# Batch 0 of an attention and maxout-FFN kernel: softmax sums inverted together on ScalarE, value bursts and three loads moved

## The chip, the cores and the metric

The kernel runs on 1 core of a Trainium2 chip. The metric is the device time of one execution in microseconds. The kernel before took 287.16 us, the median of 3 runs (286.48 to 287.23). One more execution was taken with the hardware profiler; every row of a profile shown here comes from that execution.

## The reference

```python
B, H, S, Nb, D = 8, 8, 576, 16, 64               # batches, heads, tokens, beacons, head size
k_all = concat([beacon_k, k], axis=2)            # 592 keys: 16 beacons, then the tokens
v_all = concat([beacon_v, v], axis=2)
scores = q @ k_all.T / sqrt(D)
scores = where(causal, -1e9, scores)             # beacons are seen by every query
a = softmax(scores)
attn = a @ v_all
x = attn.transpose(0, 2, 1, 3).reshape(4608, 512)
h = maximum(maximum(x @ w1, x @ w2), x @ w3)     # 512 -> 768
out = h @ w_out                                  # 768 -> 512
```

Inputs and output are float32; the kernel multiplies in bfloat16.

## The kernel before

Heads go in pairs, 4 pairs per batch, 32 pairs in all. Two pairs make a quad (4 heads), two quads a batch. The queries and keys of a pair are transposed on TensorE (`turn_part` by halves of 288 tokens in batch 0, `turn_pair` whole afterwards), each transposition into a PSUM bank that another engine copies to `qT` and `kT`. `emit_scores` multiplies keys by queries for one of four groups of key tiles and query ranges; ScalarE turns the group into exponentials in `at_sb`; `emit_masks` clears what lies above the diagonal, on VectorE or on GpSimd (POOL). `emit_pv` makes a value burst of one quad and one half of its queries: pass 0 multiplies the exponentials by ones, which gives the softmax sums, passes 1 to 3 multiply them by the even and odd columns of the values, for each of the five key tiles that the half sees. `invert_sums` makes 1/sum and `multiply` writes sum-normalised columns to `xT`, the input of the FFN. The FFN works in units; its first six are each a 256-column half of the first 512 tokens for two of six blocks of `w1`, and `emit_ffn` lets a unit through only when its tokens are in `xT`.

There is no scheduler: the order in which the Python calls stand is the order on each engine. An engine works through its own instructions in that order, and an instruction that waits holds up everything behind it. The order of batch 0 is written out by hand in `first_batch`, with `S_` for scores, `T` for a half transposition (its last argument is a number of filler matmuls of 512 columns put in front), `M` for masks (True: on VectorE), `P` for a value burst, `V` for the cast of a value tile, `F` for FFN units.

PSUM has eight banks in batch 0: scores take banks 0, 1 and 2, 3 in turn (`sc_psum`), value bursts banks 4 and 5 (`pv_psum`), FFN units banks 6 and 7 (`ffn_psum`); `emit_pv(..., apart=True)` takes the FFN's two banks, `tiles=` takes a pair of score banks. The transpositions of batch 0 name their banks 4 to 7 themselves.

Loads without a cast are issued on SyncE's queue (SP). `load_cast` (a pair of heads, as bfloat16), `load_w(i)` (FFN weight number i of three, from 0, in two halves) and `load_w_out` are issued by POOL, in its order among casts and masks, and use a DMA queue of their own. Five value tiles of 128 keys (the last of 80) come on SP's queue, issued at L306; `cast_first_v` (`V`, L334) casts each on POOL. `second_batch` goes through pairs 4 to 7, in the same way but with whole bursts of scores, and issues `load_cast(8)`, `load_w_out` and `load_cast(9)` on the way; pair 8 is transposed at its end.

Lines that the prediction speaks of: L247, L334, L277 and L322 casts, L258 `load_cast`, L344 `load_w`, L415 filler matmuls, L427 half transpositions, L435 their copies, L505 scores of batch 0 and L514 their exponentials, L558 and L560 masks on VectorE and POOL, L609 the value bursts of batch 0, L678 the reciprocal on VectorE, L680 and L681 the inversion on ScalarE (logarithm, then exponential of its negative), L691 the products, L750 and L764 the first FFN units and their casts or maxima.

Of the kernel before, what the change touches and what calls it, by code (L numbers as in the profile page):

```python
# [11 lines left out]
AF = mybir.ActivationFunctionType  # L12
# [5 lines left out]
def kernel(  # L18
# [13 lines left out]
    nc = tc.nc  # L32
# [4 lines left out]
    scale = 1.0 / float(D) ** 0.5  # L37
# [13 lines left out]
    HALF = S // 2  # L51
# [9 lines left out]
    PPB = H // 2  # L61
# [76 lines left out]
    sc_psum = Banks(0, 2, 2)  # L138
# [115 lines left out]
    def load_cast(p):  # L254
        b, g, j0 = place(p)
        for i, src in enumerate((q, k)):
            t16 = quads[g][i][:, 2 * j0 : 2 * j0 + 4]
            nc.gpsimd.dma_start(  # L258
                out=t16.rearrange("p (h s) r d -> p h (s r d)", h=2),
                in_=src[b, head(g, j0) : head(g, j0) + 2].rearrange("h (p r) d -> p h (r d)", r=QR),  # L260
            )
            rows = t16.rearrange("p (h s) r d -> p h (s r) d", h=2)
            stage["pair16", p, i] = (rows[:, 0], rows[:, 1])
# [26 lines left out]
    def load_v(b, piece, gate=None):  # L290
        st = new_stage(("v", b, piece))
        if gate:
            gate.memset(st[:, 0:1], 0.0)
        t_lo, t_hi = V_PIECES[piece]
        for t in range(t_lo, t_hi):
            i = t - t_lo
            dst = st[:, i * H * D : (i + 1) * H * D].rearrange("p (h d) -> p h d", h=H)
            lo = 0
            if t == 0:
                lo = Nb  # L300
                nc.sync.dma_start(
                    out=dst[0:Nb], in_=beacon_v[b].rearrange("h n d -> n h d")
                )
            t0 = k_tok[t] + lo
            n = k_rows[t] - lo
            nc.sync.dma_start(  # L306
                out=dst[lo : lo + n], in_=v[b, :, t0 : t0 + n, :].rearrange("h p d -> p h d")
            )
# [32 lines left out]
    def load_w(i, gs=range(n_quad)):  # L341
        wv = (moe_w1, moe_w2, moe_w3)[i].rearrange("(g p e) f -> g p e f", g=n_quad, e=2)
        for g in gs:
            nc.gpsimd.dma_start(out=w_in[i][:, 2 * g : 2 * g + 2], in_=wv[g])  # L344
# [6 lines left out]
    def load_beacons(b0, b1, dst, queue=None):  # L351
        for b in range(b0, b1):
            (queue or nc.sync).dma_start(
                out=dst[Nb * (b - b0) : Nb * (b - b0 + 1)],
                in_=beacon_k[b].rearrange("h n d -> n h d"),
            )

    def turn_beacons(b0, b1, src):
        n = Nb * (b1 - b0)
        ps = sc_psum.tile(BF16)[:, 0, 0 : PPB * n].rearrange("p (i n) -> p i n", i=PPB)  # L360
        for pi in range(PPB):
            nc.tensor.transpose(
                ps[:, pi],
                src[:, 2 * pi : 2 * pi + 2].rearrange("p h d -> p (h d)"),
                ident[0:n, 0:n],
            )
        if b0 == 0:
            by_act(kTs[0][:, 0:Nb], ps[:, 0, 0:Nb])
        by_act(bT[:, :, Nb * b0 : Nb * b1], ps)
# [43 lines left out]
    def fill(at_bank, n):  # L413
        for _ in range(n):
            nc.tensor.matmul(  # L415
                acc[:, at_bank], busy[:, 0:128], busy, start=True, stop=True
            )
# [162 lines left out]
    unfinished = []  # L580
# [87 lines left out]

        return finish

    def invert_sums(dve=False):
        if not unfinished:
            return
        quad, hf = unfinished.pop(0)
        ps = pv_tiles.pop((quad, hf))
        recip = nrm_pool.tile([128, S], FP32, name="recip")[:, 0:HALF]
        if dve:
            nc.vector.reciprocal(recip, ps[0][:, 0:HALF])  # L678
        else:
            nc.scalar.activation(out=recip, in_=ps[0][:, 0:HALF], func=AF.Ln)  # L680
            nc.scalar.activation(out=recip, in_=recip, func=AF.Exp, scale=-1.0)  # L681
        for n in range(1, NPASS):
            products.append((quad, hf, n, ps, recip))

    def multiply(count=NPASS):
        for _ in range(min(count, len(products))):
            quad, hf, n, ps, recip = products.pop(0)
            b, g = divmod(quad, n_quad)
            c0 = b % RING * S + hf * HALF
            part, bank, lo, ca, cb = passes[hf][n]  # L690
            nc.vector.tensor_mul(  # L691
                xT[:, 2 * g + part - 1, c0 + ca : c0 + cb],
                ps[bank][:, lo : lo + cb - ca],
                recip[:, ca:cb],
            )
            if g == n_quad - 1 and n == NPASS - 1:
                ready[0] = 2 * b + hf

    def finish_pv():
        invert_sums()  # L700
        multiply()

    hTs = {}
    MID = TOKB // 2
# [127 lines left out]
    def emit_ffn(limit, new_ps=ffn_psum.tile, close=False):  # L834
        if not may_emit(limit):
            return False
        need, fn, args = units[done[0]]
        done[0] += 1
        fn(*args, new_ps, *([True] if close else []))
        return True  # L840
# [72 lines left out]
    S_, T, M, P, V = emit_scores, turn_part, emit_masks, emit_pv, cast_first_v  # L913

    def F(n=1, new_ps=ffn_psum.tile, close=False):
        for _ in range(n):
            assert emit_ffn(END, new_ps, close)

    def first_batch():
        S_(0, 0)  # L920
        T(2, 0, 0, 6)
        T(3, 0, 0, 4)
        load_v(0, 0, nc.vector)
        load_v(0, 1)
        load_beacons(1, B_PE, bk32_1)
        S_(1, 0)
        T(2, 0, 1, 7)
        T(3, 0, 1, 5)
        M(0, 0, True)
        S_(2, 0)  # L930
        T(0, 1, 0, 6, None, 2)
        T(1, 1, 0, 4)
        S_(3, 0)
        T(0, 1, 1, 7, None, 2)
        T(1, 1, 1, 5)
        M(1, 0, True)
        S_(0, 1)
        V(0)
        T(2, 1, 0, 6, None, 2)
        T(3, 1, 0, 4)  # L940
        S_(1, 1)
        M(2, 0, True)
        V(1)
        load_w(0, [0])
        T(2, 1, 1, 7, None, 2)
        T(3, 1, 1, 5)
        M(3, 0, True)
        S_(0, 3)
        V(2)
        load_w(0, [1])  # L950
        S_(0, 2)
        fill(6, 2)
        S_(1, 3)
        for p in range(PPB):
            M(p, 1)
        M(0, 3, True)
        M(0, 2, True)
        V(3)
        V(4)
        load_w(1, [0])  # L960
        S_(1, 2)
        fill(6, 2)
        S_(2, 1)
        M(1, 3, True)
        M(1, 2, True)
        S_(3, 1)
        P(0, 0)
        invert_sums(True)
        multiply()
        S_(2, 3)  # L970
        load_w(1, [1])
        M(2, 3)
        P(1, 0, apart=True)
        invert_sums(True)
        multiply()
        S_(2, 2)
        M(2, 2)
        S_(3, 3)
        M(3, 3, True)
        P(0, 1, 0, 2)  # L980
        S_(3, 2)
        P(0, 1, 2)
        M(3, 2, True)
        by_pool(bk16_1, bk32_1)
        load_cast(PPB)
        load_cast(PPB + 1)
        load_cast(PPB + 2)
        load_w(2)
        load_cast(PPB + 3)
        invert_sums()  # L990
        multiply()
        P(1, 1, tiles=sc_psum.tile())
        invert_sums()
        F()
        multiply()
        F(2)
        turn_beacons(1, B_PE, bk16_1)
        place_beacons(PPB, by_act)
        F(2)
        free_banks[:] = [4, 5, 0, 1, 2, 3, 7, 6]  # L1000
        turn_pair(PPB, by_act)
        load_v(1, 0, nc.vector)
        load_v(1, 1)
        F(1, next_psum)

    def second_batch():
        for p in range(PPB, 2 * PPB):
            place_beacons(p + 1, by_act)
            emit_burst(p)
            if p == PPB + 1:  # L1010
                load_cast(2 * PPB)
            if p == PPB + 2:
                load_w_out()
                load_cast(2 * PPB + 1)
            for gi in range(NG):
                emit_masks(p, gi)
                if p == PPB + 2 and gi == 1:
                    cast_v(1, 0, by_pool)
            if p == PPB + 2:
                next_load(gate=nc.gpsimd)  # L1020
                next_load(4)
                cast_v(1, 1, by_pool)
            if p + 1 < 2 * PPB:
                turn_pair(p + 1, by_dve)
                F(2, next_psum)
                if p < PPB + 2:
                    F(1, last_pair(), True)
        F(2, next_psum)
        finish = emit_pv_whole(n_quad)
        turn_pair(2 * PPB, by_dve)  # L1030
        F(2, next_psum)
        finish()
# [93 lines left out]
```

## Time and profile before

| what | value |
|---|---|
| median of 3 runs | 287.16 us |
| the profiled execution | 286.96 us |
| its span, first to last instruction | 285.3 us |
| granted TensorE clock | 1.00 |
| TensorE busy, 9.04 to 14.43 us | 5.39 of 5.39 us |
| TensorE busy, 14.43 to 17.57 us | 2.32 of 3.14 us |
| TensorE busy, 17.57 to 22.16 us | 3.69 of 4.59 us |
| TensorE busy, 22.16 to 25.81 us | 2.73 of 3.65 us |
| TensorE busy, 25.81 to 30.86 us | 4.89 of 5.05 us |

The five stretches run from the third score group of batch 0 to the first transposition of pair 4. Columns of a timeline row: start in us from the span's start, length in us, engine, line, operation, output and input, partitions by elements, count, and in brackets the idle time of the engine before it with what ended it. PE is TensorE, PEld its weight loads, DVE is VectorE, ACT is ScalarE. Rows of one kind that follow each other closely are merged (x12 and the like), so a merged row's length is that of the whole run. Landing times are counted from the start of a DMA's issue to the arrival of its last part. q0 is the DMA queue of POOL's loads, q1 that of SP's.

### The profile page before, as it was taken

How to read it: one execution, taken by the hardware profiler on the slowest of the kernel's cores; microseconds unless marked ns; L12 is line 12 of the kernel's file. 1: busy time of each engine (PE TensorE's matmuls, PEld its weight loads, DVE VectorE, ACT ScalarE, POOL GpSimd, SP SyncE). 2: the span in 40 equal slices, each digit the busy share in tenths (PEclk: the TensorE clock that was granted, in tenths of full speed). 3: DMA queues.
4: the chain of work that ended last, by engine and by line, in shares of the span. 5: the costliest groups of instructions: out<-in, count | busy, mean ns of one | idle time of the engine just before them, and what ended most of it. 6: DMA issues, size and time to landing. Idle time of an engine off the chain costs nothing.

```text
span 285.3 us, 7780 instructions
## 1 busy us (share of the span) xinstructions
PE 275.6 (97%) x3079; PEld 157.6 (55%) x3079; DVE 177.3 (62%) x313; ACT 158.7 (56%) x295; POOL 134.4 (47%) x277
## 2 busy tenths in 40 slices
PE   7978999899999999999999999999999999999994
PEld 3447774555556555555556787555555554444442
DVE  3887675564774748373836384638364847776872
ACT  3893568885668585858585857576766640000000
POOL 7076479348386774557465836584336210000000
PEclk9999999999999999999999999999999999999999
DMA  8979999999995999999999999999861003103004
GB/s 138 207 128 184 206 219 195 229 219 289 274 165 145 241 268 228 165 252 267 240 179 231 250 238 224 179 217 237 138 177 70 0 2 112 38 0 147 2 0 147
DMA packets 85316, 48.84 MB, mean 171 GB/s; under 512 B 64416, under 2 KB 80032, under 8 KB 85280
## 3 DMA queue, kind: packets, MB, share of 16 engines
q1 hardware_dynamic: 78176, 42.22, 66.7%
q0 software_dynamic: 6544, 5.80, 13.3%
q8 instruction: 24, 0.39, 0.6%
q10 hardware_dynamic: 560, 0.33, 0.5%
q14 instruction: 12, 0.10, 0.1%
HBM read 35.13 MB, written 14.22 MB: 173 GB/s over the span
## 4 chain that ended last, share of the span: by engine, by line
PE 81%; DVE 1%; issue 1%; DVEq 0%
PE acc L721 45%; PE acc L773 16%; PE acc L642 11%; PE acc L520 7%; PE acc L406 2%; PE acc L791 0%; DVE hT L739 0%; DVE y L798 0%; DVE qT L442 0%; DVE kT L453 0%; DVEq L453 0%
## 5 line engine op out<-in xcount | busy, mean ns | idle before, releaser
L721 PE MATMUL acc<-xT,w_sb 128*128 128x512 bf16 (+4 forms) x744 | 135.5, 338 | 0.1
L739 DVE TENSOR_TENSOR hT<-hT,acc 128x512 bf16<-128x512 bf16 x102 | 69.9, 687 | 58.6 <-PE acc L721 53.7
L721 PEld LDWEIGHTS <-w_sb 128*128 128x128 bf16 x744 | 69.2, 98 | 59.6
L560 POOL TENSOR_SCALAR_AFFINE_SELECT at_sb<-at_sb 128x256 bf16<-128x256 bf16 (+1 forms) x171 | 62.2, 385 | 81.3 <-ACT at_sb L538 81.1
L538 ACT ACTIVATE at_sb<-acc 128x208 bf16<-128x208 f32 (+3 forms) x140 | 89.5, 735 | 6.8 <-PE acc L520 5.5
L773 PE MATMUL acc<-w_out_sb,hT 128*128 128x512 bf16 (+2 forms) x246 | 48.4, 348 | 0.0
L780 DVE COPY y<-acc 128x512 f32<-128x512 f32 (+1 forms) x35 | 22.0, 629 | 21.9 <-PE acc L773 15.7
L277 POOL CAST p<-st 96x768 bf16<-96x768 f32 x44 | 35.0, 824 | 0.0
L773 PEld LDWEIGHTS <-hT 128*128 128x128 bf16 x246 | 22.6, 98 | 21.7 <-DVE hT L739 1.6
L741 ACT CAST hT<-acc 128x352 bf16<-128x352 f32 x18 | 8.1, 452 | 47.0 <-PE acc L721 47.0
L741 DVE CAST hT<-acc 128x512 bf16<-128x512 f32 (+1 forms) x48 | 26.6, 554 | 9.5 <-PE acc L721 9.3
L520 PE MATMUL acc<-qT,kT 64*128 64x208 bf16 (+1 forms) x336 | 26.6, 280 | 0.5 <-DVE hT L764 0.2
L798 ACT COPY y<-acc 128x320 f32<-128x320 f32 x1 | 0.4, 426 | 46.0 <-PE acc L791 46.0
L642 PE MATMUL acc<-at_sb,v_sb 128*32 128x512 bf16 (+5 forms) x672 | 23.0, 281 | 0.6 <-issue 0.6
L520 PEld LDWEIGHTS <-kT 64*128 64x128 bf16 x336 | 15.4, 94 | 12.7 <-issue 2.6
L665 DVE TENSOR_TENSOR xT<-raw,recip 128x576 bf16<-128x576 f32 x28 | 21.1, 795 | 0.0
L642 PEld LDWEIGHTS <-v_sb 128*32 128x32 bf16 (+1 forms) x672 | 14.7, 96 | 7.4 <-issue 0.7
L322 POOL CAST v_sb<-st 128x1536 bf16<-128x1536 f32 (+2 forms) x21 | 18.3, 896 | 0.0
L652 ACT COPY raw<-acc 128x512 f32<-128x512 f32 x28 | 15.8, 633 | 2.6 <-PE acc L642 2.4
L642 PE MATMUL acc<-at_sb,ones 128*32 128x512 bf16 (+3 forms) x336 | 14.9, 284 | 0.0
L514 ACT ACTIVATE at_sb<-acc 128x1024 bf16<-128x1024 f32 (+2 forms) x16 | 13.2, 864 | 3.1 <-PE acc L505 3.1
L453 DVE COPY kT<-acc 128x576 bf16<-128x576 bf16 x12 | 9.0, 753 | 5.7 <-PE acc L406 4.5
(74 smaller groups left out, 181.8 us busy)
## 6 DMA issues: line engine op xcount, KB each, us to landing
out_dram<-y SPq DMA_DIRECT2D x35, 256.0 KB, 3.6
st<-in_q_dram SPq DMA_DIRECT2D x22, 288.0 KB, 4.3
st<-in_k_dram SPq DMA_DIRECT2D x22, 288.0 KB, 4.5
st<-in_v_dram SPq DMA_DIRECT2D x24, 256.0 KB, 6.4
w_sb<-in_moe_w_dram POOLq DMA_DIRECT2D x6, 384.0 KB, 7.7
q_dram<-p SPq DMA_DIRECT2D x16, 144.0 KB, 2.3
k_dram<-p SPq DMA_DIRECT2D x16, 144.0 KB, 2.2
st<-in_v_dram SPq DMA_DIRECT2D x8, 224.0 KB, 5.6
```

Of the source, the lines that this page charges most:

```text
L277: cast(t16.rearrange("p r h d -> p h r d"), st[0:QP, i * NQ2 : (i + 1) * NQ2].rearrange("p (h r d) -> p h r d", h=2, r=QR),)
L322: cast(v_sb[0:n, t:t1].rearrange("p t h d -> p (t h d)"), st[0:n, (t - t_lo) * H * D : (t1 - t_lo) * H * D],)
L520: nc.tensor.matmul(ps, kTs[p % NT][hs, 128 * t : 128 * t + 128], qTs[p % NT][hs, q0:q1], start=True, stop=True, tile_position=(64 * e, 0),)
L538: nc.scalar.activation(out=both_heads(p, gi)[:, e0:e1], in_=acc[:, first + e0 : first + e1, 0 : g_width(p, gi)], func=AF.Exp, scale=scale,)
L560: nc.gpsimd.affine_select(out=view, in_=view, compare_op=ALU.is_ge, fill=0.0, base=x0, pattern=[[0, 2], [1, hi - lo]], channel_multiplier=-1,)
L642: nc.tensor.matmul(acc[32 * j : 32 * j + 32, bank, lo + q0 - qa : lo + qb - qa], lhsT, at_view(PPQ * quad + j // 2, t, j % 2, q0, qb), sta ...
L665: nc.vector.tensor_mul(xT[:, 2 * g + i, c0 : c0 + S], raw[:, i], recip)
L721: nc.tensor.matmul(ps[:, a:b], w_in[i][:, ct, 128 * ft : 128 * (ft + 1)], xT[:, ct, x0 : x0 + b - a], start=(ct == 0), stop=(ct == n_ct - 1),)
L739: nc.vector.tensor_max(h[:, lo:hi], h[:, lo:hi], ps[:, lo:hi])
L741: (by_act if hi < TOKB else by_dve)(h[:, lo:hi], ps[:, lo:hi])
L773: nc.tensor.matmul(ps[:, lo:hi], hT[:, ft, 128 * tt : 128 * (tt + 1)], w_out_sb[:, ft, lo:hi], start=(ft == 0), stop=(ft == n_ft - 1),)
L780: (by_act if hi < d_model else by_dve)(y[:, lo:hi], ps[:, lo:hi])
```

## The change

`invert_sums` loses its choice of engine and takes the quad and half it is to invert; it always uses ScalarE. All four inversions of batch 0, each with its products on VectorE, stand at the end of the batch, in the order (quad 0, half 0), (1, 0), (0, 1), (1, 1); the first FFN unit stands after the third. Before, (0, 0) and (1, 0) were inverted by VectorE's reciprocal directly behind their value bursts, (0, 1) and (1, 1) by ScalarE.

Quad 0's first value burst uses the FFN's two banks, its second banks 4 and 5; quad 1's two bursts stand behind all scores and use the two pairs of score banks. The second burst of quad 0 starts in front of the last-but-one score group and not behind it. Four transpositions of batch 0 have one filler matmul in front where they had two. The two halves of `load_w(0)` are asked one place sooner each, in front of the casts V(1) and V(2); the two of `load_w(1)` move among calls of other engines. `load_cast(8)` moves from pair 5's turn to pair 6's, ahead of `load_w_out`.

```diff
-    def invert_sums(dve=False):
-        if not unfinished:
-            return
-        quad, hf = unfinished.pop(0)
+    def invert_sums(quad, hf):
+        unfinished.remove((quad, hf))
         ps = pv_tiles.pop((quad, hf))
         recip = nrm_pool.tile([128, S], FP32, name="recip")[:, 0:HALF]
-        if dve:
-            nc.vector.reciprocal(recip, ps[0][:, 0:HALF])
-        else:
-            nc.scalar.activation(out=recip, in_=ps[0][:, 0:HALF], func=AF.Ln)
-            nc.scalar.activation(out=recip, in_=recip, func=AF.Exp, scale=-1.0)
+        nc.scalar.activation(out=recip, in_=ps[0][:, 0:HALF], func=AF.Ln)
+        nc.scalar.activation(out=recip, in_=recip, func=AF.Exp, scale=-1.0)
...
-        T(0, 1, 0, 6, None, 2)
+        T(0, 1, 0, 6, None, 1)
         T(1, 1, 0, 4)
         S_(3, 0)
-        T(0, 1, 1, 7, None, 2)
+        T(0, 1, 1, 7, None, 1)
...
         V(0)
-        T(2, 1, 0, 6, None, 2)
+        T(2, 1, 0, 6, None, 1)
         T(3, 1, 0, 4)
+        load_w(0, [0])
         S_(1, 1)
         M(2, 0, True)
         V(1)
-        load_w(0, [0])
-        T(2, 1, 1, 7, None, 2)
+        load_w(0, [1])
+        T(2, 1, 1, 7, None, 1)
...
         V(2)
-        load_w(0, [1])
...
         V(4)
-        load_w(1, [0])
         S_(1, 2)
...
         S_(3, 1)
-        P(0, 0)
-        invert_sums(True)
-        multiply()
+        load_w(1, [0])
+        P(0, 0, apart=True)
         S_(2, 3)
         load_w(1, [1])
         M(2, 3)
-        P(1, 0, apart=True)
-        invert_sums(True)
-        multiply()
         S_(2, 2)
         M(2, 2)
+        P(0, 1, 0, 2)
         S_(3, 3)
         M(3, 3, True)
-        P(0, 1, 0, 2)
+        P(0, 1, 2)
         S_(3, 2)
-        P(0, 1, 2)
         M(3, 2, True)
...
         load_cast(PPB + 3)
-        invert_sums()
-        multiply()
+        P(1, 0, tiles=sc_psum.tile())
         P(1, 1, tiles=sc_psum.tile())
-        invert_sums()
-        F()
-        multiply()
+        for quad, hf in ((0, 0), (1, 0), (0, 1), (1, 1)):
+            invert_sums(quad, hf)
+            multiply()
+            if (quad, hf) == (0, 1):
+                F()
         F(2)
...
-            if p == PPB + 1:
+            if p == PPB + 2:
                 load_cast(2 * PPB)
-            if p == PPB + 2:
                 load_w_out()
                 load_cast(2 * PPB + 1)
```

More of the change, by code (lines that the diff above doesn't have):

```diff
@@ L697, in multiply @@
                 ready[0] = 2 * b + hf
-    def finish_pv():
-        invert_sums()
-        multiply()
     hTs = {}
@@ L989, in first_batch @@
         load_cast(PPB + 3)
-        invert_sums()
-        multiply()
+        P(1, 0, tiles=sc_psum.tile())
         P(1, 1, tiles=sc_psum.tile())
-        invert_sums()
-        F()
-        multiply()
+        for quad, hf in ((0, 0), (1, 0), (0, 1), (1, 1)):
[3 more added lines that the diff above has]
+                F()
         F(2)
```

## The prediction

> **What bounds the kernel now.** First the page: its engine rows and the chain that ended last.
>
> ```profile
> PE 275.6 (97%) x3079; PEld 157.6 (55%) x3079; DVE 177.3 (62%) x313; ACT 158.7 (56%) x295; POOL 134.4 (47%) x277
> PE 81%; DVE 1%; issue 1%; DVEq 0%
> ```
>
> TensorE is busy 275.6 of 285.3 us, and by the view of waits its matmuls wait 1.0 us in all after 31 us, never for a DMA. From there the kernel is a row of matmuls that starts when batch 0 lets it start; the change edits batch 0 and one load behind it, so I read its timeline. In the first half:
>
> ```profile
> 11.85 0.60 PE L415 MATMUL acc<-busy 128*128 128x512 bf16 x2
> 11.96 1.02 ACT L514 ACTIVATE at_sb<-acc 128x1024 bf16<-128x1024 f32 x1 [0.21 <-PE acc L505]
> 12.38 0.45 PE L427 MATMUL acc<-ident,quad 96*64 96x96 bf16 x12
> 12.76 0.39 PE L505 MATMUL acc<-qT,kT 64*128 64x288 bf16 x4
> 13.19 1.02 ACT L514 ACTIVATE at_sb<-acc 128x1024 bf16<-128x1024 f32 x1 [0.21 <-PE acc L505]
> ```
>
> Columns: start, length, engine, line. One step (two fills, 12 transposes, one score group) takes TensorE 13.19 - 11.96 = 1.23 us; the exp takes 1.02 and waits 0.21 for TensorE. TensorE sets this pace, with filler matmuls in it. In the second half:
>
> ```profile
> 18.31 1.96 DVE L678 RECIPROCAL recip<-acc 128x288 f32<-128x288 f32 x1 [0.38 <-PE acc L609]
> 20.26 0.39 PE L505 MATMUL acc<-qT,kT 64*128 64x288 bf16 x4 [0.46 <-ACT at_sb L514]
> 21.06 0.68 PE L609 MATMUL acc<-at_sb,ones 128*32 128x288 bf16 x20 [0.41 <-DVE xT L691]
> 21.17 1.95 DVE L678 RECIPROCAL recip<-acc 128x288 f32<-128x288 f32 x1
> 22.87 0.41 ACT L680 ACTIVATE recip<-acc 128x288 f32<-128x288 f32 x1
> 23.31 0.44 ACT L681 ACTIVATE recip<-recip 128x288 f32<-128x288 f32 x1
> 24.31 0.56 PE L609 MATMUL acc<-at_sb,ones 128*32 128x288 bf16 x10 [0.92 <-DVE at_sb L558]
> 25.81 2.86 PE L750 MATMUL acc<-xT,w_sb 128*128 128x256 bf16 x24
> 29.03 1.91 PE L750 MATMUL acc<-xT,w_sb 128*128 128x256 bf16 x16 [0.16 <-DVE hT L764]
> ```
>
> Two reciprocals hold VectorE for 3.9 us. Behind the first stand the products that free PSUM banks 4 and 5 (TensorE waits 0.41), behind the second the masks of pair 3 (0.92). ScalarE inverts a half in 0.41 + 0.44 = 0.88 us with the gap. Last the DMAs, by window:
>
> ```profile
> q1 hardware_dynamic: 64, 0.02, 8.0%
> q1 hardware_dynamic: 987, 0.24, 72.7%
> q0 software_dynamic: 166, 0.40, 105.1%
> 15.65 0.70 POOL L334 CAST v_sb<-st 128x512 bf16<-128x512 f32 x1 [1.43 <-DMA st<-in_v_dram]
> 16.30 0.56 POOL L344 DMA_DIRECT2D w_sb<-in_moe_w_dram  x1
> ```
>
> Columns: packets, MB, share of 16 engines. At 15.0 to 15.9 us the value loads run at 8%, one engine of the 16 that lags; at 16.0 to 17.5 the fifth value tile (160 KB, issued 12.64, landed 5.6 later, 18.2) and beacons pass alone. At 33.4 to 35.4 only the weight queue moves, although a value load was issued at 32.77.
>
> **The change, part by part.**
>
> *Fills.* Four pairs become single: 4 x 0.21 = 0.85 us off TensorE's steps from 9.4 to 14.4. A step becomes 1.02 and the exps then run back to back, so nothing is lost; VectorE (4.63 busy of 5.39 us there) has its copies 0.4 us earlier and no score group waits for them. The exp of 14.43 starts at 13.6, that of 17.38 at 16.54. What fills cover is TensorE's clock, granted 1.00 in every stretch here; were it lost, the 480-column fills of the first microseconds (3.38 / 8 = 0.42 against 0.21 us for 512 columns now) say 5 us of work doubles: at most +4. I take 0.
>
> *The scores' half.* Quad 0's first burst goes to banks 6 and 7, so its second burst waits for no product; quad 1's first moves behind the scores. No matmul is added. From 16.54: the exps of S(2,1) and S(3,1) end at 18.5, S(2,2) follows to 18.8, the 40 matmuls of P(0,1,0,2) last 1.1 as at 21.06 to 22.16 and end at 19.9 instead of 22.16, if the value tiles are there.
>
> *The value tiles.* `load_w(0)` moves on POOL's queue: its first half stands behind V(0), at 14.2 instead of 16.30, its second in front of V(2), at 16.35 instead of 17.40. (Both calls for index 1 move past no other POOL instruction, so that queue keeps V(3), V(4), weight 1, masks: the weight asked sooner is index 0.) In front of V(1) the issue costs nothing: V(1) waits for its DMA to 15.65 anyway. But its packets come 1.3 us after the issue (none before 17.5 now), so at 15.5, and the fifth tile reaches the engines at 16.0, behind them. A half is 128 packets, 8 per engine; the 105 of 17.6 to 19.7 give 16 x 2.1 x 0.88 / 105 = 0.28 us each, so 2.2 us per half. Idle engines finish it at 17.7 and the tile lands at 18.6: no loss. On the lagging engine either its value ring goes on first (again 18.6), or the half does after the third and fourth tiles: 17.0 + 2.2 + 0.6 + 0.3 = 20.1, V(4) ends at 20.7 and P(0,1,0,2) at 20.8, 0.9 late. Rows for going on are few (17.6 to 18.0), for first come the 33.4 row; I take the middle, +0.4, so P(0,1,0,2) ends at 20.3. V(4) late also makes weight 1 and the masks of pair 2 late by as much: 22.8 at worst, and P(1,1) needs them at 23.0.
>
> *The inversions.* From 20.3: S(3,3) to its exp 0.42 (20.26 to 20.68), exps 1.0 + 0.4, to 22.1; two inversions of 0.88, to 23.9; three products of (1,0), 0.88 (23.22 to 24.11), to 24.75. P(1,0) and P(1,1) (0.8 + 1.7 us of matmuls) run beside this from 21.7 to 24.2. The first FFN unit can then finish 5 of its 8 matmuls at 0.12: 25.35, against 25.81 + 1.0 = 26.8. The products of (0,1) and the unit's cast (0.88 + 0.69) stand ahead of those of (1,1) (0.88, to 27.15) and of the second cast (27.85), which frees bank 7 for the fourth unit: 27.85 instead of 29.03. Gain 1.2 us. Weight 0 landed at 24.5 (17.40 + 7.1) and now sooner, so it isn't the bound.
>
> *What carries it.* Pair 4's `load_cast` landed at 30.1 for a transposition at 30.86. Its queue is served in order behind the weights, which run up to 2 us earlier, so it lands near 28, needed at 29.6. Cost 0; without the earlier weight 0 it would cut the gain to 0.7.
>
> *Pair 8.* 1.3 us of POOL issue (0.65 + 0.63 at 36.92) pass from pair 5's masks to before pair 6's; POOL comes to it at 41.51 - 1.2 = 40.3, its second piece goes out at 41 and lands 8 us later, at 49, needed at 50.44 - 1.2 = 49.2. Batch 1's value casts end at 48.05 now and its bursts need the last of them near 49.5, a slack of 1.4 us, of which the 1.3 of issue take all but 0.1. Cost 0, between -0.2 (a freer value load) and +0.4.
>
> Sum: 286.96 - 1.2 = 285.7 us, the profiled execution's time (its span 285.3); it lies 0.2 under the median 287.16.
>
> **Rivals.**
>
> *A, the values starve (slower).* If the engines alternate between the two queues, the lagging one puts each weight half (2.2 us) between short runs of value packets: the third tile, now 16.5, lands near 20.5. V(2) ends at 21.1, P(0,0) at 21.3, the exps of S(2,3), S(2,2) at 23.0, S(3,3)'s at 24.5, S(3,2)'s at 24.9, two inversions 26.65, products 27.5, first unit 28.1 instead of 26.8: 286.96 + 1.3 = 288.2. It decides once the third tile lands after about 18.5. For it: the lagging engine, POOL's order. Against: at 33.4 to 35.4 the waiting queue got nothing at all, so no turns were taken there.
>
> [...]
>
> *B, given back later.* The gain arrives at 29.6 but POOL's 1.3 us or pair 8's landing (issue to landing 6.1 to 8.3 in such rows) holds TensorE near 49 us: 286.96 - 1.2 + 0.9 = 286.7. For it: POOL is full from 43.6 to 49.9 us. Against: the slack above.
>
> *C, the clock drops* for lack of fills: +3, 290. Against: filler and scores are still 0.6 of a step.
>
> **Chances.** Forecast with both ends of its value term (0 and 0.9 late: 285.3 to 286.2) 0.61; A 0.22; B 0.14; C 0.03. Its own range, with the 0.2 to the median, is 285.0 to 286.4. To leave out no more than 2 in 10 the range goes to 288.0, most of A, from 285.0. A measurement of this kernel tells about 0.3% (0.86 us) from no change: faster is the forecast but for its late end, and little else: 0.57; same is that end and B, 0.19; slower is A and C, 0.24.
>
> **What would show it.** Exps 1.02 to 1.05 us apart from 9.5 to 13.6; no RECIPROCAL; P(0,1,0,2) ending between 19.9 and 20.8; the last value cast ending between 19.2 and 20.7; the first L750 row near 24.3, the fourth unit near 27.9; bursts at 48.2 now near 47. Wrong if V(2)'s cast waits past 18.5 us, if the L750 row starts after 25.8, or if TensorE waits for a `quad` or `v_sb` after 28 us.

## The result, and the profile after

| | median | range | executions |
|---|---|---|---|
| before | 286.73 us | 286.06 to 287.67 | 11 |
| changed | 285.16 us | 284.70 to 287.34 | 11 |

The ratio is 0.995 (95% interval 0.9927 to 0.9973): faster by 0.5%, some 1.4 us. Executions more than 1.5% above the fastest of the same kernel are left out of every ratio here, but not of the medians; the profiled ones of `w1late`, `pair8old` and `shift` are among them.

The profiled execution of the changed kernel took 286.59 us (span 284.9), one of the two longest of the eleven. Its page, engine rows and chain:

```profile
PE 274.5 (96%) x3075; PEld 157.3 (55%) x3075; DVE 173.7 (61%) x311; ACT 159.9 (56%) x299; POOL 134.2 (47%) x277
PE 81%; DVE 1%; issue 0%; DVEq 0%
```

TensorE sets the end as before, with 1.1 us less work. VectorE has lost the two reciprocals (313 instructions before, 311 now). The timeline of ScalarE and POOL, then of TensorE, in batch 0:

```profile
9.31 5.39 ACT L514 ACTIVATE at_sb<-acc 128x1024 bf16<-128x1024 f32 x6 [0.15 <-PE acc L505]
19.48 0.61 POOL L334 CAST v_sb<-st 80x512 bf16<-80x512 f32 x1 [2.03 <-DMA st<-in_v_dram]
```

```profile
21.77 0.40 PE L609 MATMUL acc<-at_sb,ones 128*32 128x288 bf16 x12 [0.30 <-ACT at_sb L514]
21.99 0.63 PE L609 MATMUL acc<-at_sb,v_sb 128*32 128x288 bf16 x28
22.44 0.63 PE L609 MATMUL acc<-at_sb,ones 128*32 128x288 bf16 x14
25.03 0.27 PE L609 MATMUL acc<-at_sb,ones 128*32 128x208 bf16 x4 [1.96 <-DVE xT L686]
25.16 1.18 PE L609 MATMUL acc<-at_sb,v_sb 128*32 128x288 bf16 x54
26.27 2.86 PE L739 MATMUL acc<-xT,w_sb 128*128 128x256 bf16 x24
29.49 1.91 PE L739 MATMUL acc<-xT,w_sb 128*128 128x256 bf16 x16 [0.16 <-DVE hT L753]
```

The exponentials run back to back (six rows of ScalarE merged into one). V(4)'s cast waits for the fifth value tile until 19.48. Then something stands here that neither the kernel before nor the prediction has: TensorE stops in the middle of P(1,1), from 22.8 to 25.03 us. The first FFN unit (L739 here, L750 before; its casts are L753) starts at 26.27, later than the 25.81 of before. The bracket puts the stop down to VectorE's products, L686. VectorE's own timeline speaks against it:

```profile
21.75 0.76 DVE L558 TENSOR_TENSOR at_sb<-at_sb,tri 128x160 bf16<-128x160 bf16 x3 [4.77 <-ACT at_sb L514]
22.83 1.68 DVE L686 TENSOR_TENSOR xT<-acc,recip 128x288 bf16<-128x288 f32 x6 [0.32 <-ACT recip L676]
```

The last masks, the only thing of VectorE's that P(1,1) reads, end at 22.51, and P(1,1) writes to banks that the products at 22.83 do not read. (L675 and L676 are the inversion on ScalarE, L686 the products.) What was under way while TensorE stood still, by DMA queue from 22.7 to 23.8 us (packets, MB, share of 16 engines):

```profile
q0 software_dynamic: 87, 0.22, 106.8%
q8 instruction: 1, 0.02, 5.4%
q1 hardware_dynamic: 2, 0.00, 0.2%
```

One packet of the instruction queue stands among 87 of the weights. The whole page has 24 such packets, 0.39 MB, so 16 KB each, for 6150 records of TensorE (weight loads and matmuls): about 256 records a packet. So I take a packet to be TensorE's next block of code, an inference from these counts.

A second profile of the changed kernel (the run `again`) took 285.17 us, next to the median of 285.16, and has no stop:

```profile
22.91 0.75 PE L609 MATMUL acc<-at_sb,ones 128*32 128x288 bf16 x20
23.45 1.21 PE L609 MATMUL acc<-at_sb,v_sb 128*32 128x288 bf16 x56
24.59 3.12 PE L739 MATMUL acc<-xT,w_sb 128*128 128x256 bf16 x24
28.07 1.91 PE L739 MATMUL acc<-xT,w_sb 128*128 128x256 bf16 x16 [0.15 <-DVE hT L753]
29.90 0.70 PE L406 MATMUL acc<-ident,quad 96*64 96x96 bf16 x24
```

Its batch 0 began 0.51 us later than that of before (the third exponential at 9.99 against 9.48), so for a comparison with before 0.51 is to be taken off: first FFN unit 24.08 against 25.81, fourth unit 27.56 against 29.03, first transposition of pair 4 29.39 against 30.86.

### The profile page after: what moved, and what is told of

Same layout as the page of the kernel before. It is cut to its first block, busy times and chain, and to the rows that moved or that the text cites. A ratio compares the mean times of both kernels' runs of the same rounds, so it can differ in the third digit from the quotient of the medians.

```text
span 284.9 us, 7772 instructions
## 1 busy us (share of the span) xinstructions
PE 274.5 (96%) x3075; PEld 157.3 (55%) x3075; DVE 173.7 (61%) x311; ACT 159.9 (56%) x299; POOL 134.2 (47%) x277
## 4 chain that ended last, share of the span: by engine, by line
PE 81%; DVE 1%; issue 0%; DVEq 0%
PE acc L710 45%; PE acc L762 16%; PE acc L642 11%; PE acc L520 7%; PE acc L406 2%; PE acc L780 0%; DVE hT L728 0%; DVE y L787 0%; DVE qT L442 0%; DVE kT L453 0%; DVEq L453 0%
## 5 line engine op out<-in xcount | busy, mean ns | idle before, releaser
L762 PEld LDWEIGHTS <-hT 128*128 128x128 bf16 x246 | 22.6, 98 | 21.7 <-DVE hT L728 1.6
L642 PE MATMUL acc<-at_sb,v_sb 128*32 128x512 bf16 (+5 forms) x672 | 22.8, 281 | 0.0
```

The source lines that it names most:

```text
L642: nc.tensor.matmul(acc[32 * j : 32 * j + 32, bank, lo + q0 - qa : lo + qb - qa], lhsT, at_view(PPQ * quad + j // 2, t, j % 2, q0, qb), sta ...
L762: nc.tensor.matmul(ps[:, lo:hi], hT[:, ft, 128 * tt : 128 * (tt + 1)], w_out_sb[:, ft, lo:hi], start=(ft == 0), stop=(ft == n_ft - 1),)
```

## The experiments

Two theories of the stop. Theory 1: TensorE waits for its own instructions, whose packet waits among other DMAs. Theory 2: it waits for VectorE, as the bracket says. "Record" counts TensorE's weight loads and matmuls in the order of their starts, from 0; where a trace lacks a record or two, a stop at 703 shows as 701. A stop's length is counted from the start of the last record in front of it to the start of the first one behind it, so it is a little longer than the idle time in brackets.

**again**: the changed kernel, a second profile.

> The changed kernel once more, for a second profile. Theory 1 (instruction fetch): TensorE goes on 2.2 to 2.4 us after the fetch's packet starts, whenever that is, and the packet's start differs between executions by what stands ahead of it among the DMAs: if it starts at 20.3 or sooner there is no stop in front of record 703 and the span is near 283.4; if at 22.8, the stop is 2 us again. Theory 2 (a wait for VectorE): VectorE's masks and products are no later in one execution than in another, so the stop is there again with 2 us. Time 284.7 to 285.7, ratio to before 0.995.

Ratio 0.993 (0.9907 to 0.9954), median 284.95. The packet started at 20.91 and TensorE reached record 703 at 23.33 without a stop. VectorE's masks ended at 23.39 and its products at 24.99: the matmul that "waited for the products" at 25.03 in the first profile ran here before most of them, and before the last mask had ended. So it doesn't depend on the products, and theory 2 falls for them.

**w1late**: weight 1 behind pair 5's load.

```diff
-        load_w(1, [0])
         P(0, 0, apart=True)
         S_(2, 3)
-        load_w(1, [1])
...
         load_cast(PPB + 1)
+        load_w(1)
         load_cast(PPB + 2)
```

> Both halves of weight 1 are asked behind pair 5's load and no longer in front of batch 0's last bursts; nothing needs weight 1 before about 36 us. Theory 1 (the new stop of TensorE in P(1,1), 22.8 to 25.0 us in the changed kernel, is its fetch of instructions, one 16 KB packet that started only at 22.78 because weight packets were ahead of it): with fewer of them in the ring the packet starts at 22 us or sooner, the stop in front of the 703rd TensorE record (weight loads and matmuls counted together) shrinks from 2.2 us to 1.2 or less, the first FFN unit starts by 25.5, time 284.3 to 284.9. Theory 2 (the stop is a wait for VectorE, as the bracket of its row says: the masks of pair 3 or the products): VectorE's work does not change, the stop stays at about 2 us, time 285.2.

The packet started at 21.90, the stop was 1.14 us (23.02 to 24.16) and the first FFN unit started at 25.40, as theory 1 said; VectorE's six products ended 0.2 us later than in the changed kernel (24.71 against 24.51), while the stop ended 0.87 sooner. But the time is no better (median 287.91, ratio 0.9968, 0.9933 to 1.0003). In the profiled execution, 293.67 us, one of four over 292, this is why: with weight 1 later, SP's issue of batch 1's third value tile took 5.47 us (3.56 in the changed kernel), the fifth was issued at 42.56 and not 40.41, only 0.33 us ahead of `w_out`, and landed at 54.04 (45.41). TensorE waited 5 us for it. In the two profiles of the changed kernel, with weight 1 asked sooner, the tile is issued 2.4 and 2.75 us ahead of `w_out` and TensorE does not wait for it.

**w0old**: weight 0 at its places of before.

```diff
-        load_w(0, [0])
         S_(1, 1)
...
         V(1)
-        load_w(0, [1])
+        load_w(0, [0])
...
         V(2)
+        load_w(0, [1])
```

> Weight 0's halves go back to their places of before, behind V(1) and V(2). The prediction's term: its packets no longer meet the fifth value tile, V(4) ends at about 19.3 instead of 20.1 and P(0,1,0,2) at 19.9 instead of 20.3. Theory 1 (instruction fetch behind weight packets): weight 0 and weight 1 now stand in the ring together at 19 to 23 us, so the packet of instructions starts no sooner than 21.8, the stop at record 703 stays at 1 to 2.5 us and eats the 0.4; time 285.0 to 285.6. Theory 2 (VectorE): masks and products come 0.3 to 0.4 sooner and so does the end of the stop; time 284.8.

Ratio 0.9997 (0.9964 to 1.0029), above the range expected. In its profile (287.05 us) the masks and products came sooner than in the changed kernel, and the stop was longer, 2.92 us:

```profile
22.18 0.63 PE L609 MATMUL acc<-at_sb,ones 128*32 128x288 bf16 x14
25.48 0.27 PE L609 MATMUL acc<-at_sb,ones 128*32 128x208 bf16 x4 [2.67 <-DVE xT L686]
```

The packet started at 23.14. Theory 2's 284.8 did not come. This profile is the second fastest of the twelve executions and the median is 288.15. Ten of the twelve have a mean granted clock of 0.987 to 0.994, against one of eleven of the changed kernel (0.994, its 287.34 us). A stop that costs the clock, as those of 3.04 us and more did and the 2.92 us of this profile did not (last section), would make such executions, but none of them was profiled. So the times speak for weight 0 asked sooner, which the prediction charged with 0.4 us for the value tile (0.995 and 0.993 against 0.9997, though the first interval overlaps this one); the clock is a likely reason, not a shown one.

**shift** and **shift64**: 64 more TensorE instructions at the start, no DMA and no data changed.

```diff
-        keep_busy(8, 480)
+        keep_busy(40, 96)
```

> The first eight filler matmuls of 480 columns become forty of 96: the same columns, 32 more matmuls, so 64 more TensorE instructions ahead of everything. Theory 1 (a boundary of instruction blocks): the stop is again in front of record 703, which is now 32 matmuls earlier in the program, in P(1,0) and not in P(1,1), though P(1,0) waits for none of the masks of the last group. Theory 2 (data): the stop stays in front of the 15th matmul of P(1,1), now record 767. Time by both within 0.7 of 285.2.

Ratio 0.9925 (0.9899 to 0.9951), the time as expected by both. Its profiled execution took 709.25 us, so where the stop stands can't be read from it. The same shift with 32 columns of weights in each filler (`keep_busy(40, 96, m=32)`, the output and the weights cut to m) was shift64:

> The changed kernel with the first eight fillers as 40 of 96 columns on 32 columns of weights: 64 more TensorE instructions ahead, half of what the run with 72 had. Theory 1: the second block's fetch is then asked near 17 us and needed near 22.2, 5.2 us later (4.0 in the changed kernel, 2.9 us for the third block where 128 more were ahead), so a delay of up to 2.9 us ahead of the packet and the 2.3 behind it fit in: no stop over 0.4 us from 20 to 30 us. Time 284.3 to 284.9, a ratio to before of 0.990 to 0.993, with fewer long runs. If block boundaries don't matter, it is the changed kernel's 0.993 to 0.995.

```profile
21.95 0.40 PE L609 MATMUL acc<-at_sb,v_sb 128*32 128x288 bf16 x10
23.67 0.43 PE L609 MATMUL acc<-at_sb,v_sb 128*32 128x48 bf16 x18 [1.32 <-issue]
```

The stop, 1.51 us, is now in P(1,0), in the middle of its 28 value matmuls, in front of the same record, 32 matmuls sooner in the program. Nothing of P(1,0) waits for VectorE there, and the profile names no releaser ("issue"). This places the stop in the stream of instructions, not in the data, and theory 2 falls for the masks too. The expected cure did not come: the block was begun at 17.64, its packet went out 3.61 us later, more than the 2.9 I allowed, and the ratio is 0.9952 (0.9931 to 0.9973).

**nomask**: the masks of pair 3's last two score groups left out.

```diff
-        M(3, 3, True)
+        masked.add((3, 3))
...
-        M(3, 2, True)
+        masked.add((3, 2))
```

> The masks of pair 3's last two score groups, on VectorE, are left out (part of the causal mask is not applied). Theory 1: the stop of P(1,1) stays, in front of record 703, until the fetch is done, near 24 to 25 us. Theory 2, masks: P(1,1) runs from 22.4 to 24.1 without a stop over 0.3 us. Theory 2, products: they begin 0.3 to 0.7 sooner and the stop ends as much sooner. Time 285.2 by theory 1, 284.0 by theory 2.

No stop, median 285.28, ratio 0.9916 (0.9883 to 0.995, four executions). By the letter of it the missing stop is theory 2's and the time theory 1's, but the packet started at 19.75 in this execution, so theory 1 has no stop either. With `again`, which keeps the masks and has no stop, it tells nothing.

**early**: 128 more instructions.

```diff
-        keep_busy(8, 480)
+        keep_busy(72, 54, m=32)
```

> The first eight fillers of 480 columns become 72 of 54 columns on 32 columns of weights: about the same columns, 64 more matmuls, 128 more TensorE instructions ahead of everything. No DMA and nothing on VectorE changes. Theory 1: every boundary comes 64 matmuls sooner in the program, so the fetch is asked near 15 us, ahead of most weight packets, and its block is needed at about 21 us: the packet starts before 18.5, no stop over 0.5 us in P(1,1) or in front of record 703; time no longer than the changed kernel's, 284.4 to 285.2, with less spread. Theory 2: the stop in P(1,1) stays at 0.9 to 2 us, time as the changed kernel's.

Right about P(1,1), wrong about the time: ratio 1.0067 (1.0044 to 1.009). The packet started at 18.94, not before 18.5, but still 2.24 us ahead of record 703. The stop there is gone, and a longer one stands in front of record 958, where the next block begins, in the first FFN unit:

```profile
23.95 0.39 PE L739 MATMUL acc<-xT,w_sb 128*128 128x256 bf16 x2
27.28 4.20 PE L739 MATMUL acc<-xT,w_sb 128*128 128x256 bf16 x22 [2.93 <-issue]
```

This block was begun at 21.18, the packet went out at 24.99, while weight 1 was moving, and the quick matmuls of P(1,1) were through the block by 24.1. I had worked out the second boundary and not the third. The stop also cost the clock: by windows (columns: TensorE, its weight loads, VectorE, ScalarE, POOL; then the granted clock, DMA share, GB/s)

```profile
24.00:27.00 3.00, 0.34 (x5) 0.06 (x2) 1.44 (x6) 1.47 (x4) 3.00 (x6) 1.00 1.05 145
27.00:30.00 3.00, 2.72 (x13) 1.94 (x14) 1.22 (x3) 0.00 (x0) 1.50 (x3) 0.54 1.22 177
```

22 matmuls took 4.20 us where 24 take 2.86 in the changed kernel.

**nostream** and **stream2**: fewer and more weight packets when the block is asked.

```diff
-        load_w(0, [1])
...
-        load_w(1, [0])
...
-        load_w(1, [1])
...
         load_cast(PPB + 1)
+        load_w(0, [1])
+        load_w(1)
```

The other way round, stream2 has weight 1 up front:

```diff
         load_w(0, [1])
+        load_w(1)
...
-        load_w(1, [0])
...
-        load_w(1, [1])
```

> Weight 0's second half and both of weight 1 are asked behind pair 5's load, so that between the landing of weight 0's first half and pair 4's load no weight packets move. The first FFN unit then waits for weight 0 until about 32 us, so the time (290 to 296) tells nothing; the fetch does. Theory 1 with the weights as what stands ahead of the packet: from the 447th record of TensorE (where the block before begins) to the packet 0.3 to 1.4 us, as for the first block at 11 us; no stop in front of record 703. If something else than the weights delays it: 1.5 to 4 us.

0.70 us from record 447 to the packet, no stop; the wait for weight 0 is the 7.6 us of the last row:

```profile
22.41 0.68 PE L609 MATMUL acc<-at_sb,ones 128*32 128x288 bf16 x20
22.90 1.19 PE L609 MATMUL acc<-at_sb,v_sb 128*32 128x288 bf16 x56
32.02 1.89 PE L739 MATMUL acc<-xT,w_sb 128*128 128x256 bf16 x8 [7.61 <-DMA w_sb<-in_moe_w_dram]
```

> Both halves of weight 1 are asked right behind weight 0's second half, in front of V(2): more weight packets are in the ring before the block is asked near 19 us. Theory 1: from record 447 to the packet 4 us or more, a stop of 2.2 us or more in front of record 703, and TensorE goes on 2.2 to 2.4 us behind the packet's start. If the weights don't delay it: 0.7 to 4.0 us as in the four profiles of this order of instructions.

3.62 us to the packet and a stop of 1.97 us, TensorE on 2.44 behind the packet: long, but inside the 0.7 to 4.0 that profiles of this order of instructions had, so this run does not show that more weights delay it more.

The profiles of the changed kernel's order together, for the block that begins at record 703 (times in us; "begun" is the start of the block before, record 447, and "resumes" the start of record 703; "weights" is the landing of weight 0's second half, in `early` of weight 1's):

| run | begun | packet | waited | resumes | packet to resume | stop | weights |
|---|---|---|---|---|---|---|---|
| changed | 18.77 | 22.78 | 4.01 | 25.03 | 2.25 | 2.21 | 23.25 |
| w0old | 19.18 | 23.14 | 3.96 | 25.48 | 2.34 | 2.92 | 24.11 |
| stream2 | 18.99 | 22.61 | 3.62 | 25.05 | 2.44 | 1.97 | 22.79 |
| shift64 | 17.64 | 21.25 | 3.61 | 23.68 | 2.43 | 1.51 | 23.27 |
| w1late | 19.12 | 21.90 | 2.78 | 24.16 | 2.26 | 1.14 | 22.34 |
| early, next block | 21.18 | 24.99 | 3.81 | 27.28 | 2.29 | 3.20 | 25.73 |
| again | 19.45 | 20.91 | 1.46 | 23.33 | 2.42 | none | 21.65 |
| pair8old | 19.45 | 20.45 | 1.00 | 23.07 | 2.62 | none | 22.24 |
| fills2 | 19.60 | 20.41 | 0.82 | 22.98 | 2.57 | none | 21.34 |
| nomask | 19.07 | 19.75 | 0.68 | 22.89 | 3.14 | none | 21.20 |
| nostream | 18.91 | 19.61 | 0.70 | 22.79 | 3.18 | none | 31.98 |

In these six stops TensorE goes on 2.25 to 2.44 us after the packet starts, in P(1,1), in P(1,0) or in the first FFN unit; where the packet is early, there is none. That is shown. What makes the packet wait 0.7 us in one profile and 4.0 in another is not: the weight queue was moving meanwhile (the 106.8% above), and with no weights it waited 0.70, but that is one profile, and four with the same weights as the changed kernel (again, pair8old, fills2, nomask) waited 0.7 to 1.5. The last column tells the two kinds apart (in nostream that half was issued only at 23.98, behind the packet). Where weight 0's second half landed 2.8 us or less after the block was begun (those four), the packet waited 0.7 to 1.5 us; where it landed 3.2 us or more after (the first five rows, the block at 703 in `early`, the kernel before and `fills`), 2.4 to 4.0. That fits a packet that waits behind weights, but both may be late for one common reason, and no run parts the two.

**pair8old**: pair 8's load back in pair 5's turn.

```diff
-            if p == PPB + 2:
+            if p == PPB + 1:
                 load_cast(2 * PPB)
+            if p == PPB + 2:
                 load_w_out()
```

> The changed kernel with pair 8's load back in pair 5's turn. The prediction priced this move at nothing (-0.2 to +0.4): time within 0.4 of the changed kernel. Its rival B said that pair 8's load, late, holds batch 1's bursts near 49 us: then this is faster by 0.3 to 1.5. The opposite, that the early pair 8 stands ahead of batch 1's last value tile, would make this one slower: TensorE then waits for POOL's value cast (L322) at 48 to 50 us.

Median 286.17, ratio 0.9962 (0.993 to 0.9994); the times spread from 284.88 to 289.3, where `again`, on the same chip, went from 284.38 to 286.39. In the profiled execution (289.3 us) the third outcome happened; POOL, then TensorE:

```profile
50.55 0.61 POOL L322 CAST v_sb<-st 80x512 bf16<-80x512 f32 x1 [3.66 <-DMA st<-in_v_dram]
```

```profile
51.22 1.03 PE L642 MATMUL acc<-at_sb,v_sb 80*32 80x80 bf16 x20 [2.79 <-POOL v_sb L322]
```

The fifth value tile of batch 1, issued at 39.72, landed at 50.50, after `w_out` (issued 40.26). In `again` it was issued at 39.31, `w_out` only at 41.74, behind the two issues of pair 8, and it landed at 44.52. So the moved load can be a guard for the tile: its issues keep the 768 KB of `w_out` further behind the tile's. Over all the profiles but shift's, the tile landed 4.1 to 6.6 us behind its issue where that was 1.86 us or more ahead of `w_out` (the kernel before, 2.06, and `fills`, 1.86, included, though they load pair 8 early), and 10.8 and 11.5 us behind where it was 0.54 (pair8old) and 0.33 us (w1late). By the ratios alone the move's worth is not shown: the intervals of pair8old and `again` overlap.

**fills** and **fills2**: the single fillers alone in the kernel before, and the changed kernel with the fillers doubled again.

```diff
-        T(0, 1, 0, 6, None, 2)
+        T(0, 1, 0, 6, None, 1)
...
-        T(2, 1, 1, 7, None, 2)
+        T(2, 1, 1, 7, None, 1)
```

> The kernel before with the four pairs of fillers made single and nothing else. The prediction's term: 0.85 us less of TensorE's steps up to 14.4 us, clock still 1.00; if batch 0's second half keeps its length, time 285.9. Theory 1: the second half is then bound by the fetch as before, whose packet comes no sooner than the weights let it, and the masks of pair 3; part of the 0.85 is lost there: 285.9 to 286.6. Theory 2: the second half has only waits for VectorE, all of which move with it: 285.9.

Ratio 0.9964 (0.9947 to 0.9982), median 285.93, as expected. The profile (286.38 us) shows less of a gain than that. In it the exponential of 14.43 comes 0.86 us sooner against the third one (14.09 - 10.00, before 14.43 - 9.48), but the fourth FFN unit only 0.36 (29.19 - 10.00, before 29.03 - 9.48). The rest is lost in front of P(0,1) and in P(1,1), so the whole 0.85 is not seen to arrive:

```profile
20.96 0.68 PE L609 MATMUL acc<-at_sb,ones 128*32 128x288 bf16 x20 [0.65 <-DVE xT L691]
24.21 0.30 PE L609 MATMUL acc<-at_sb,ones 128*32 128x288 bf16 x4 [0.92 <-DVE at_sb L558]
24.73 0.27 PE L609 MATMUL acc<-at_sb,ones 128*32 128x208 bf16 x4 [0.22 <-DVE at_sb L558]
```

The wait for the products behind the reciprocal has grown from 0.41 to 0.65 us, and behind the mask's 0.92 stands a further 0.22 that ends 2.41 us after the packet (22.32): by theory 1 the fetch, which in the kernel before lies under the wait for the mask.

> The changed kernel with the four pairs of fillers as before: the order of the bursts, the inversions and the loads alone. The prediction's terms (fillers 0.85 of a gain of 1.2) would leave 0.35 of the gain here: ratio to before 0.998 to 1.000. The fillers alone gave 0.9964, the whole change 0.993 to 0.995: if both parts add up, this one gives 0.997 to 0.999, 286.3 to 287.0. By theory 1 its second block is asked later against the weights and the stop in P(1,1) may be as in the changed kernel, 0 to 2 us.

Ratio 0.9945 (0.9923 to 0.9967), median 285.51: more than expected, as much as the whole change. Against the third exponential the fourth FFN unit comes 1.08 us sooner than before (27.86 - 9.39 against 19.55), with single fillers, in `again`, 1.47 (28.07 - 9.99). So in these profiles the order, the inversions and the loads are worth 1.1 us and the fillers add 0.4; no run parts the order of the bursts from the inversions on ScalarE. With double fillers no value burst waits for V(4); with single ones TensorE gets there first and waits for it. The expectation had taken the fillers' full 0.85 off without giving back the value tile's 0.4.

None of the runs is shown to beat the changed kernel: shift, at 0.9925, and nomask, at 0.9916 with work left out, lie within an interval of its two measurements.

## Why the prediction was right, step by step

Times of `again` less its 0.51 us of later start stand against the forecast, since that execution lies at the median and has no stop.

- *Fills.* Forecast 13.6 and 16.54 for the exponentials of 14.43 and 17.38, and clock 1.00. Measured 13.57, 16.52 and 1.00. Right, and rival C did not happen for lack of fillers. C's price doesn't come out of its own numbers: 5 us of work doubled is 5, and the text has "at most +4" and then +3. Nor is the clock shown behind the 0.42 us of the first fillers, from which C takes its doubling: the windows of the kernel before have no lower clock there (1.00 from 0 to 5 us). Where the clock was lost, in `early` (0.54 from 27 to 30 us), the 4.20 us for 22 matmuls are some 1.6 more than at the changed kernel's pace.
- *Value tiles.* Forecast V(4) ending 19.2 to 20.7 and P(0,1,0,2) at 20.3, the tile 0.4 late. Measured 20.04 and 20.31; the fifth tile landed 1.1 us later than before (19.37 against 18.23). The cast V(2) stood without a wait at 16.3, far from the 18.5 at which rival A decides. From 15.5 to 16.5 us of `again` the value queue moved 71 packets at 7.9% while the weights ran at 98.7%: no slower than the 64 at 8.0% that the prediction shows without them. The turns between the two queues that rival A assumes, which would have starved the third tile, made no such time here.
- *Inversions.* Forecast exponentials done 22.1, two inversions 23.9, products 24.75, fourth unit 27.85. Measured 21.97, 23.52, 24.48 and 27.56. The mechanism is right; two inversions took 1.66 us and not 1.8, and began while the exponentials were ending (the rows are not shifted by 0.51):

```profile
21.18 1.30 ACT L514 ACTIVATE at_sb<-acc 128x992 bf16<-128x992 f32 x2 [1.02 <-PE acc L505]
22.37 0.42 ACT L675 ACTIVATE recip<-acc 128x288 f32<-128x288 f32 x1
23.59 0.44 ACT L676 ACTIVATE recip<-recip 128x288 f32<-128x288 f32 x1
23.32 1.67 DVE L686 TENSOR_TENSOR xT<-acc,recip 128x288 bf16<-128x288 f32 x6
```

  The gain up to the fourth unit, fillers included, is 1.47 us, forecast 1.2.
- *Pair 4.* Forecast near 28, needed 29.6. Measured 27.8 and 28.4, needed 29.39; no wait.
- *Pair 8.* Forecast issue 40.3, landing 49, cost 0. Measured 39.97, its second piece landed at 44.88, 4.3 us behind its issue and not 8. Batch 1's burst was at 46.62 (forecast near 47), and TensorE's matmuls have no wait over 0.2 us from 28 to 60 us. Rival B did not happen. But "Cost 0, between -0.2 (a freer value load) and +0.4" may be the wrong price: in one execution, pair8old's profile, a stop of 3 us stood where the move was undone, because `w_out` came close behind the value tile. I had asked only whether pair 8 comes too late, not what its issues hold back.
- *The sum.* Forecast 285.7, measured 285.16. Some of the difference may not be of the change: in the kernel before's profile a stop stands near 57 us, in front of record 1727, four blocks behind 703, between matmuls of one kind with no releaser:

```profile
56.31 0.22 PE L642 MATMUL acc<-at_sb,v_sb 128*32 128x64 bf16 x6
57.09 0.21 PE L642 MATMUL acc<-at_sb,v_sb 128*32 128x64 bf16 x2 [0.56 <-issue]
```

  Its packet started at 54.08, so TensorE went on 3.02 us after it, a little longer than in the six stops. These 0.56 us are over half of the 1.0 us of waits after 31 us that the prediction put down as "never for a DMA".

- *What was missing.* The prediction called itself wrong "if the L750 row starts after 25.8": in the first profile it started at 26.27, and that execution, 286.59 us, was only 0.4 us shorter than the profiled one before. The forecast holds for the median, next to which lies the profile without a stop. It had no term for the fetch, so as far as the stop goes it came out right by luck. The step that failed is "P(1,0) and P(1,1) (0.8 + 1.7 us of matmuls) run beside this from 21.7 to 24.2". They do when their instructions are there. In the kernel before, the wait for the mask to 24.2 us lay over the same fetch (packet at 21.80, record 703 at 24.31), so that no wait in it was put down to the fetch; with the mask's wait gone the fetch may be the last thing to end. In the two profiles of the changed kernel it took back 2.2 us and nothing.

Most crossings from one block to the next cost little: in each profile but shift's at most two of the crossings after the first have a stop over 0.25 us, but six profiles have one of 1.1 to 3.2 us. In the profiles of the kernel before and the changed one the packet of a block goes out from 5.8 us ahead of the beginning of the block before to 4.0 us behind it.

## What to carry to other kernels

When a wait is removed, ask what else was ending under it: here, by all the runs show, a fetch of instructions that the wait for the mask had covered (packet at 21.80, mask to 24.2, record 703 at 24.31). In batch 0's stretch of small matmuls 256 records ran in 4 us (18.77 to 22.82 in the changed kernel), and in the six profiles with a stop the packet of the next block went out 2.8 to 4.0 us after the block's beginning and TensorE went on 2.25 to 2.44 us behind it. The bracket named VectorE's products in four of the six and nothing ("issue") in `shift64` and `early`; the test is to move the instruction stream without touching data and see whether the stop stays with the record or with the data. A load that is moved for its own need can also shift the loads issued behind it (`w_out` at 41.74 in `again`, 40.26 in pair8old), and that may be worth more than the need: in pair8old's profile TensorE waited 2.79 us for the value tile.

## What the runs showed of the hardware

- The stops of TensorE of 3.04 us and more cost more than themselves. Around the end of the stop the granted clock was 0.63 from 51 to 54 us in pair8old (stop of 3.04 us), 0.54 from 27 to 30 in early (3.20), 0.63 from 52 to 56 and 0.51 from 56 to 60 in w1late (5.23), 0.50 from 32 to 36 in nostream (7.88); in w0old, with a stop of 2.92 us, it was 1.00 from 20 to 34. In the traces of pair8old and early it is 0.5 for one stretch of 3.41 us, which over the whole execution makes a mean of 0.994, an estimate (1 - 0.5 x 3.41 / 285; the two executions have 0.994 and 0.993). For pair8old:

```profile
48.00:51.00 3.00, 0.43 (x12) 0.11 (x4) 0.00 (x0) 0.00 (x0) 0.45 (x1) 1.00 1.20 256
51.00:54.00 3.00, 2.78 (x62) 2.02 (x63) 0.32 (x1) 2.19 (x6) 1.99 (x7) 0.63 1.13 242
```

- The instruction queue moved 24 packets of 16 KB (0.39 MB) in an execution with 6150 records of TensorE, about 256 records a packet. In batch 0's dense stretch a packet started 0.7 to 4.0 us after the block before was begun, and in the six stops of 1.14 to 3.20 us the first instruction behind the stop ran 2.25 to 2.44 us after the packet's start (3.02 us in the stop of the kernel before near 57 us).
